# Seven products for two more groups of the first strip, and evictions by a bounded addition and a square

## The chip, the cores and the metric

The kernel runs on one core of a Trainium2 chip. A core has TensorE (matrix products, into the banks of PSUM), VectorE, ScalarE and GpSimd (elementwise work, named DVE, ACT and POOL in the profile), and SyncE (SP), which issues nearly all transfers of this kernel. Each engine has a queue of its own and works through it in order; semaphores tie the queues together. The metric is device time in microseconds, and lower is better. The kernel before took 870.62 us (median of three runs, 869.41 to 871.22).

## The reference

```
kv  = einsum('bhsd,bhse->bhde', k, v)          # batch 8, heads 8, seq 576, head_dim 64
o   = einsum('bhsd,bhde->bhse', q, kv)
rms = sqrt(mean(o * o, axis=-1) + 1e-6)
x   = (o / rms * g_norm) as (4608, 512)        # tokens x (heads * head_dim)
h   = x @ w_in                                 # w_in (512, 2048), given as float64
g   = max(h, 0) ** 2
out = g @ w_out                                # w_out (2048, 512), given as float64
```

All of it is computed in fp32 from k, v, q in fp32. The two products of the feed-forward part are nearly all of the arithmetic.

## The kernel before

**Strips.** The 4608 tokens are worked in 9 strips of 512. For each strip the kernel computes h, squares it and multiplies by w_out ("up" and "down"). Between these products TensorE does the attention of later strips in small slices, in an order that Python code writes out by hand; the compiled order of every engine is the order in which the code emits. TensorE's work is cut down by Strassen's scheme in Winograd's form: a product of 2 x 2 blocks by seven products of sums of blocks instead of eight. Strips 2 to 8 apply it twice, strip 1 once in up and twice in down, strip 0 once in down.

**Strip 0, up.** It uses w_in as it comes, without sums. A group g (of `NG` = 4) holds four tiles, `(fh, i)`; a tile is four matmuls with 512 columns into a bank of its own (`up_first`, tag "f", four banks in rotation), and the group's four quarters of g are the tiles `dest[11]`, `dest[12]`, `dest[21]`, `dest[22]`. ScalarE evicts a tile: relu in place (L916), then a square for each half (L918). Three tiles of group 0 are done in the opening; the other thirteen are the steps i = 3 to 15.

**Weights.** While that goes on the weights arrive as float64 and are converted to fp32 in pairs of pieces. `convert(PACE[i])`, called after each step, says how far. For each pair ScalarE makes two words (L260, L262), GpSimd clamps one (L282), and VectorE puts them together (L284, L288). ScalarE's words of pair n + 1 are emitted with the rest of pair n; a pair's word tile `w_c` has two buffers and its raw tile five. Pairs 2 to 7 are w_in (groups 1 to 3), pairs 8 to 11 quarters of w_out that go into `w_s`, and pairs 12 to 15 the other quarters, of which VectorE also makes sums (`sums_out`, L306), which SP stores to HBM.

**Down of strip 0 and what follows.** At the end of up VectorE makes sums of g (`sum_g1`, L897); `down` then runs the seven products in the order 1, 2, 5, 6, 7, 3, 4. During it ScalarE scales w_in by g_norm and VectorE makes the seven-product sums of w_in for strip 1 (`sums_in`, four operations for a group: a sum and three differences, into `w_s` and over block a21) and the sums of x of strip 1 (`sums_x`, four tiles).

**Seven products (`up`).** For a group the products come in the order 1, 2, 6, 5, 7, 3, 4 (`ORDER`), eight matmul instructions of 256 columns each. They share three banks (`BANK`): A takes 1, 6, 7 and 4, which add up in it, B takes 5 and 3, and C takes 2. `combine` reads a bank between its products: after 1, 6 and 5 ScalarE copies it out (`snap`, L880); after 2, 7 and 3 VectorE adds bank and snapshot into quarters 11, 22 and 12 (L933), and multiplies the result by its positive part (L934); after 4 ScalarE takes bank A by relu and square (L938, L939) into quarter 21. Snapshots lie in the pool "c", six buffers.

```
    ORDER = (1, 2, 6, 5, 7, 3, 4)
    BANK = {1: "A", 6: "A", 7: "A", 4: "A", 5: "B", 3: "B", 2: "C"}
    A_IN = {1: 0, 2: 2, 3: 6, 4: 3, 5: 4, 6: 5, 7: 1}
```

`A_IN` names the block of w_in that a product takes: 0 to 3 are the four blocks themselves, 4 to 6 the sums s1, s2, s4. Attention slices come between: transposes (T), products of keys and values (K), queries (x_ps), norms (root on ScalarE, newton steps and x_n on VectorE) and features.

Of the kernel before, what the change touches and what calls it, by code (L numbers as in the profile page):

```python
# [9 lines left out]

FP32 = mybir.dt.float32
I32 = mybir.dt.int32
# [2 lines left out]
AF = mybir.ActivationFunctionType  # L15
ALU = mybir.AluOpType
# [4 lines left out]
def kernel(  # L21
# [34 lines left out]
    nc = tc.nc  # L56
    P = 128
# [13 lines left out]
    TH = STRIP // 2  # L71
# [4 lines left out]
    SQ = 32  # L76
    Q_ON_PE = 2
    BEHIND = 1.6
    X_ON_PE = 2
    EPS = 1e-6  # L80
    AHEAD = 10
    PACE = (3, 4, 4, 5, 6, 7, 8, 9, 10, 11, 12, 13, 13, 14, 15, 16)
# [9 lines left out]
    c_pool = ctx.enter_context(tc.tile_pool(name="c", bufs=6))  # L92
# [124 lines left out]
    KH, FH, DH = NP // 2, d_ff // 2, d_model // 2  # L217
    FQ = FC // 2
    WN = 512
    NG = FQ // 2  # L220
# [3 lines left out]
    block = lambda b: w_in[:, :, :, b] if b < 4 else w_s[:, :, :, b - 4]  # L224
# [67 lines left out]
    def convert_pair(n, dest):  # L292

        for i in range(acted[0], min(n + 2, len(sources) // 2)):
            convert_pair_on_act(i)
            acted[0] = i + 1
        deque(conversion(pair_words.pop(n), dest, nc.gpsimd), 0)
        load_more(2 * n + 2)
# [6 lines left out]
    def minus(eng, out, a, b):  # L305
        eng.tensor_tensor(out=out, in0=a, in1=b, op=ALU.subtract)  # L306
# [3 lines left out]
    def pieces_in(i):  # L310
        g, k = divmod(i // 2, KH)
        convert_pair(i // 2, w_in[:, k, g].rearrange("p (a b) e -> p a (b e)", a=2))

    def sums_in(g):

        nc.scalar.activation(w_in[:, :, g, 0:4], w_in[:, :, g, 0:4], AF.Copy, scale=g_col)
        a11, a21, a12, a22, s1, s2, s4 = (block(b)[:, :, g] for b in range(7))
        nc.vector.tensor_tensor(out=s1, in0=a21, in1=a22, op=ALU.add)
        minus(nc.vector, s2, s1, a11)
        minus(nc.vector, s4, a12, s2)  # L320
        minus(nc.vector, a21, a11, a21)
# [24 lines left out]
    def convert(n):  # L346
        while converted[0] < min(n, len(conversions)):
            fn, a = conversions[converted[0]]
            fn(a)
            converted[0] += 1  # L350
# [339 lines left out]
    def halves(s, kh, th):  # L690
        return xt[s][:, ts(th, TH // SQ), ts(kh, KH), :]

    def sums_x(s):
        xc[s] = t1, t2, t3, t4 = [
            sum_pool.tile([P, TH // SQ, KH, SQ], FP32, name=f"x_t{i}", tag="sum") for i in range(4)
        ]
        x = lambda kh, th: halves(s, kh, th)
        minus(nc.vector, t1, x(0, 1), x(0, 0))
        minus(nc.vector, t2, x(1, 1), t1)
        minus(nc.vector, t3, x(1, 1), x(0, 1))  # L700
        minus(nc.vector, t4, x(1, 0), t2)
# [99 lines left out]
    def attend_between(slot, begun, goal, late, first, last):  # L801
# [6 lines left out]
        while slice_at[0] < most:  # L808
# [58 lines left out]
    def product(p, i, lhsT, rhs, n):  # L867

        for k in range(n):
            nc.tensor.matmul(  # L870
                bank[BANK[p]][:, i, :], lhsT=lhsT(k), rhs=rhs(k),
                start=p in (1, 5, 2) and i == 0 and k == 0, stop=k == n - 1, skip_group_check=True,
            )
# [46 lines left out]
    def up(s, g, p):  # L920
        open_bank(p)
        rhs = {
            1: halves(s, 0, 0), 2: halves(s, 1, 0), 3: halves(s, 1, 1),
            4: xc[s][3], 5: xc[s][0], 6: xc[s][1], 7: xc[s][2],
        }[p]
        for i in range(2):
            product(p, i, lambda kc: block(A_IN[p])[:, kc, g, ts(i, P)], lambda kc: rhs[:, :, kc, :], KH)
        dest = quarters(s, g)

        def relu_squared(q):  # L930
            def f(b, a):
                o = dest[q]
                nc.vector.tensor_tensor(out=o, in0=b, in1=a, op=ALU.add)  # L933
                nc.vector.scalar_tensor_tensor(out=o, in0=o, scalar=0.0, in1=o, op0=ALU.max, op1=ALU.mult)  # L934
            return f

        def last(b):
            nc.scalar.activation(dest[21], b, AF.Relu)  # L938
            nc.scalar.activation(dest[21], dest[21], AF.Square)  # L939

        combine(p, relu_squared(11), relu_squared(12), last, relu_squared(22))
# [417 lines left out]
    for s in range(N_STRIP):  # L1359
# [7 lines left out]
        if s >= DEEP_UP:  # L1367
            steps = [(0.5, up_slot, (s, slot)) for slot in range(55)]
        elif s == 0:
            steps = [(2, up_first, (g, fh, i)) for g in range(NG) for fh in range(2) for i in range(2)]  # L1370
        else:
            steps = [(1, up, (s, g, p)) for g in range(NG) for p in ORDER]
        n_up = len(steps)
# [6 lines left out]
        if s >= DEEP_UP:  # L1380
            goal = max(goal, min(ready[DEEP_UP] + (len(slices) - ready[DEEP_UP]) * (s - 1) // (N_STRIP - DEEP_UP - 1), len(slices)))
            if s > DEEP_UP:
                goal = min(pair_ends, key=lambda end: abs(end - goal))
        total, done = sum(w for w, _, _ in steps), 0
        for i, (w, fn, a) in enumerate(steps):
            if s == 0 and i < n_up:

                if i == 0:
                    load_next()
                    load_rest(1, nc.sync)  # L1390
                    load_next()
                if i == 1:
                    load_next()
                if i == 2:
                    for b in range(2):
                        load_q_rest(b, nc.sync)
                if i == 14:
                    for b in range(2):
                        store_first(b)
            elif s == 0 and i == n_up:  # L1400
                convert(len(conversions))
                conv.close()

                stream_pool = ctx.enter_context(tc.tile_pool(name="stream", bufs=6, reuse_waits="tile"))
                sum_pool = ctx.enter_context(tc.tile_pool(name="sum", bufs=8, reuse_waits="tile"))
# [6 lines left out]
            fn(*a)  # L1412
            if s == 0 and i < n_up:

                convert(PACE[i])
            done += w
            if s:
                clock[0] += 3.2 if i >= n_up else 2.2 if s == DEEP else 1.2
                soon = tiles_due and tiles_due[0][2][0] // NT == s + 1
                if i == n_up + 10:  # L1420
                    while tiles_due and tiles_due[0][2][0] // NT == s + 1:
                        _, f, a = tiles_due.popleft()
# [35 lines left out]
                sums_in((7, 8, 9, 12).index(i - n_up))  # L1458
            if i == n_up + 11:
                sums_x(1)  # L1460
            n = i + 1 - (n_up - 6)
            pairs, m = divmod(max(n - 2 * NP, 0), 3)
            attend(min(ready[0] + min(max(n, 0), 2 * NP) + (n >= 2 * NP) + 4 * pairs + (0, 2, 2)[m], goal))
            while deep_due and i not in (n_up + 1, n_up + 4, n_up + 12, n_up + 13):
# [38 lines left out]
```

## Time and profile before

| | |
|---|---|
| median of three runs | 870.62 us |
| the profiled execution | 868.8 us, span 867.0 us |
| TensorE busy | 857.8 us (99%) |
| VectorE, ScalarE, GpSimd busy | 702.0, 348.9, 328.1 us |
| granted TensorE clock | 1.000 |
| a plain tile of strip 0, start to start | 3.43 us (8 instructions) |
| a product of 256 columns in up, start to start | 1.73 us (8 instructions) |
| up of strip 0 after the opening | 33.6 to 82.4 us |
| down of strip 0 | 83.1 to 138.2 us |
| up of strip 1 | 138.25 to 195.1 us |

In the timelines a line gives start, duration, engine, line of the kernel, operation, and what is written from what; a bracket at the end gives how long the engine was idle before and what ended that. A matmul in fp32 is two instructions, and consecutive ones overlap, so the distance from start to start is the price and not the duration. ScalarE is busy for 12.9, 12.4 and 14.8 of 15 us in the stretches 30 to 45, 45 to 60 and 60 to 75 us, VectorE for 8.8, 8.6 and 12.0 there and for 14.8 and 14.6 in the next two.

### The profile page before, as it was taken

The page shows a single profiled execution, that of the slowest core. Times are in us where ns is not written, and L with a number is a line of the kernel's source. Part 1 is how long each engine was busy: PE and PEld are TensorE (multiplying, and loading weights), DVE is VectorE, ACT ScalarE, POOL GpSimd, SP SyncE. Part 2 cuts the span into 40 slices and gives each one's busy share as a digit, 9 for nine tenths or more (in the row PEclk, how much of TensorE's full clock was granted, in tenths as well). Part 3 has the DMA queues.
Part 4 walks back from the last instruction along what each step waited for, and adds up shares of the span by engine and source line. Part 5 has one row for each costly group of instructions (what it writes and reads, how often), then busy time and mean ns, then how long its engine had stood idle before and what let it go on. Part 6 is the DMA issues. An engine that isn't in the chain of part 4 may idle for free.

```text
span 867.0 us, 32426 instructions
## 1 busy us (share of the span) xinstructions
PE 857.8 (99%) x14176; PEld 804.2 (93%) x14176; DVE 702.0 (81%) x1132; ACT 348.9 (40%) x777; POOL 328.1 (38%) x335
## 2 busy tenths in 40 slices
PE   7999999999999999999999999999999999999998
PEld 6445888889999999999999999999999999999998
DVE  3768988879877996789688967897889777975887
ACT  4888241320048303750356034901491148102810
POOL 1223004630458223730574045704470447145700
PEclk9999999999999999999999999999999999999999
DMA  9898998999999997989698979987678856885583
GB/s 307 277 362 269 274 377 239 295 332 353 280 264 259 342 325 233 228 307 344 209 244 273 341 239 281 283 297 270 198 236 302 301 165 221 293 282 196 175 315 121
DMA packets 169469, 236.46 MB, mean 273 GB/s; under 512 B 78704, under 2 KB 133744, under 8 KB 161008
## 3 DMA queue, kind: packets, MB, share of 16 engines
q1 hardware_dynamic: 169024, 234.33, 83.5%
q8 instruction: 111, 1.82, 0.9%
q14 instruction: 30, 0.25, 0.1%
q10 hardware_dynamic: 304, 0.07, 0.0%
HBM read 197.66 MB, written 36.70 MB: 270 GB/s over the span
## 4 chain that ended last, share of the span: by engine, by line
PE 83%; DMA 7%; DVE 5%; ACT 3%; SPq 1%; issue 1%; DVEq 0%; ACTq 0%
PE ps_A L865 36%; PE ps_B L865 31%; PE ps_C L865 5%; PE ps_A L870 4%; DMA raw<-in_moe_w_in_dram 2%; PE kv_ps L448 2%; PE x_ps L484 2%; PE ps_B L870 2%; DVE w_t L306 1%; DMA w_deep<-w_t 1%; DMA raw<-in_moe_w_out_dram 1%; DMA w_blk<-w_deep 1%; PE ps_C L870 1%; DMA first_qkv<-in_v_dram 1%; ACT w_c L260 1%
## 5 line engine op out<-in xcount | busy, mean ns | idle before, releaser
L865 PE MATMUL ps_B<-w_blk,g_s 128*64 128x128 f32 x2016 | 122.0, 273 | 0.0
L865 PEld LDWEIGHTS ps_B<-w_blk,g_s 128*64 128x64 f32 x2016 | 112.6, 137 | 0.1
L306 POOL TENSOR_TENSOR x_l<-xT 128x256 f32<-128x256 f32 x21 | 16.2, 773 | 230.2 <-PE ps_A L865 230.2
L865 PE MATMUL ps_B<-w_blk,gt 128*64 128x128 f32 x1504 | 94.1, 273 | 0.3 <-DMA w_blk<-w_deep 0.3
L865 PE MATMUL ps_A<-w_blk,g_s 128*64 128x128 f32 x1536 | 92.2, 273 | 0.0
L1323 POOL TENSOR_TENSOR snap<-snap,gt 128x512 f32<-128x512 f32 x35 | 46.2, 1320 | 112.5 <-ACT snap L1328 93.6
L865 PEld LDWEIGHTS ps_A<-w_blk,g_s 128*64 128x64 f32 x1536 | 85.7, 137 | 0.0
L865 PEld LDWEIGHTS ps_B<-w_blk,gt 128*64 128x64 f32 x1504 | 84.6, 137 | 0.8 <-PE ps_B L865 0.5
L1328 ACT COPY snap<-ps_A 128x512 f32<-128x512 f32 x63 | 36.8, 585 | 103.6 <-PE ps_A L865 96.2
L1263 ACT ACTIVATE gt<-gt 128x512 f32<-128x512 f32 x112 | 70.2, 627 | 9.9 <-DVE gt L1323 9.9
L1264 ACT ACTIVATE gt<-gt 128x512 f32<-128x512 f32 x112 | 70.7, 631 | 3.5
L865 PE MATMUL ps_A<-w_blk,gt 128*64 128x128 f32 x1152 | 71.2, 273 | 0.0
L865 PEld LDWEIGHTS ps_A<-w_blk,gt 128*64 128x64 f32 x1152 | 64.7, 137 | 0.0
L1112 ACT COPY o_sb<-ps_A 128x128 f32<-128x128 f32 x24 | 6.4, 265 | 144.7 <-PE ps_A L865 109.4
L306 DVE TENSOR_TENSOR gt<-gt 128x2048 f32<-128x2048 f32 (+1 forms) x29 | 59.7, 2063 | 0.0
L1111 DVE TENSOR_TENSOR o_sb<-o_sb,ps_B 128x256 f32<-128x256 f32 (+1 forms) x123 | 47.4, 386 | 14.3 <-ACT o_sb L1112 9.5
L865 PE MATMUL ps_A<-x_l,w_in 128*64 128x128 f32 x896 | 58.6, 273 | 0.2 <-DVE gt L1323 0.2
L1323 POOL TENSOR_TENSOR gt<-gt,snap 128x512 f32<-128x512 f32 x42 | 52.5, 1279 | 15.1 <-DVE snap L1323 15.1
L865 PEld LDWEIGHTS ps_A<-x_l,w_in 128*64 128x64 f32 x896 | 50.8, 137 | 0.5 <-DVE gt L1323 0.5
L865 PE MATMUL ps_B<-x_l,w_blk 128*64 128x128 f32 x784 | 51.2, 273 | 0.0
L865 PE MATMUL ps_A<-x_l,w_blk 128*64 128x128 f32 x784 | 51.2, 273 | 0.0
L1112 ACT COPY o_sb<-ps_B 128x128 f32<-128x128 f32 x31 | 8.2, 265 | 96.3 <-PE ps_B L865 96.3
(214 smaller groups left out, 1900.2 us busy)
## 6 DMA issues: line engine op xcount, KB each, us to landing
w_blk<-w_deep SPq DMA_DIRECT2D x56, 1024.0 KB, 7.3
w_blk<-w_out SPq DMA_DIRECT2D x56, 768.0 KB, 6.2
w_blk<-w_in_deep SPq DMA_DIRECT2D x49, 768.0 KB, 5.8
raw<-in_moe_w_in_dram SPq DMA_DIRECT2D x16, 512.0 KB, 9.2
raw<-in_moe_w_out_dram SPq DMA_DIRECT2D x16, 512.0 KB, 8.0
k<-in_k_dram SPq DMA_DIRECT2D x29, 256.0 KB, 4.9
v<-in_v_dram SPq DMA_DIRECT2D x29, 256.0 KB, 5.2
x_d<-x_q SPq DMA_DIRECT2D x27, 256.0 KB, 4.8
```

Of the source, the lines that this page charges most:

```text
L260: nc.scalar.activation(c, high_f, AF.Copy, scale=EXPONENT)
L306: eng.tensor_tensor(out=out, in0=a, in1=b, op=ALU.subtract)
L448: nc.tensor.matmul(ps[ts(h, D), i], lhsT=a, rhs=w, start=i == 0 and c == 0, stop=c == C, skip_group_check=True)
L484: nc.tensor.matmul(ps[half, r, i, ts(p, D)], lhsT=q[row, half], rhs=kvd[b, p][row, row], start=True, stop=True)
L865: nc.tensor.matmul(ps[half], lhsT=lhsT[:, half], rhs=rhs, start=start, stop=stop, skip_group_check=True)
L870: nc.tensor.matmul(bank[BANK[p]][:, i, :], lhsT=lhsT(k), rhs=rhs(k), start=p in (1, 5, 2) and i == 0 and k == 0, stop=k == n - 1, skip_gro ...
L1111: add = lambda out, a, b: nc.vector.tensor_tensor(out=out, in0=a, in1=b, op=ALU.add)
L1112: yield nc.scalar.copy(q[:, 3:4], small(1))
L1263: nc.scalar.activation(o, o, AF.Relu)
L1264: nc.scalar.activation(o, o, AF.Square)
L1323: add = lambda eng, out, a, b: eng.tensor_tensor(out=out, in0=a, in1=b, op=ALU.add)
L1328: nc.scalar.copy(t, ps)
```

## The change

Groups 2 and 3 of strip 0 (`PLAIN` = 2) are computed by the seven products of `up`. The sums of x that it needs are made by `sums_x(0)` in four buffers of the pool "c", ahead of step 5's conversion; the sums of w_in, unscaled since strip 0's x carries g_norm, by `first_sums_in`, for group 2 ahead of step 6's conversion and for group 3 after the fourth product of group 2 (product 5) and the conversion behind it. Because `w_s` is filled with w_out at that time, s1, s2 and s4 are put into the group's own quarters 22, 12 and 21, which the products' evictions overwrite later; a11 - a21 goes over a21. `sums_in` then has three operations for groups 2 and 3, starting from that difference. The steps of strip 0's up are 8 tiles and 14 products; the variable `at` maps a product's step to one of the sixteen turns, so that loads, conversions and attention slices keep to the turns.

The evictions change in strip 1 (quarters 11, 22 and 12) and in strip 0 for quarter 12: one operation of VectorE adds bank and snapshot and bounds the sum from below by zero (`TENSOR_ADD_SAT`), and ScalarE squares it in place. In strip 0 quarters 11 and 22 keep the two operations of VectorE.

```diff
+    first_w = {}
+    def first_sums_in(g):
+        a11, a21, a12, a22 = (block(b)[:, :, g] for b in range(4))
+        dest = quarters(0, g)
+        s1, s2, s4 = first_w[g] = [dest[q] for q in (22, 12, 21)]
+        nc.vector.tensor_tensor(out=s1, in0=a21, in1=a22, op=ALU.add)
+        minus(nc.vector, s2, s1, a11)
+        minus(nc.vector, s4, a12, s2)
+        minus(nc.vector, a21, a11, a21)
...
     def sums_in(g):
...
+        if g >= PLAIN:
+            minus(nc.vector, s2, a22, a21)
+            nc.vector.tensor_tensor(out=s1, in0=s2, in1=a11, op=ALU.add)
+            minus(nc.vector, s4, a12, s2)
+            return
...
     def sums_x(s):
+        pool, tag = (sum_pool, "sum") if s else (c_pool, "c")
         xc[s] = t1, t2, t3, t4 = [
-            sum_pool.tile([P, TH // SQ, KH, SQ], FP32, name=f"x_t{i}", tag="sum") for i in range(4)
+            pool.tile([P, TH // SQ, KH, SQ], FP32, name=f"x_t{i}", tag=tag) for i in range(4)
         ]
...
         for i in range(2):
-            product(p, i, lambda kc: block(A_IN[p])[:, kc, g, ts(i, P)], lambda kc: rhs[:, :, kc, :], KH)
+            b = A_IN[p]
+            w = first_w[g][b - 4] if s == 0 and b > 3 else block(b)[:, :, g]
+            product(p, i, lambda kc: w[:, kc, ts(i, P)], lambda kc: rhs[:, :, kc, :], KH)
...
                 o = dest[q]
+                if s or q == 12:
+                    nc.vector._custom_dve(TENSOR_ADD_SAT, out=o, in0=b, in1=a, s0=float("inf"), s1=0.0)
+                    nc.scalar.activation(o, o, AF.Square)
+                    return
                 nc.vector.tensor_tensor(out=o, in0=b, in1=a, op=ALU.add)
                 nc.vector.scalar_tensor_tensor(out=o, in0=o, scalar=0.0, in1=o, op0=ALU.max, op1=ALU.mult)
...
-            steps = [(2, up_first, (g, fh, i)) for g in range(NG) for fh in range(2) for i in range(2)]
+            steps = [(2, up_first, (g, fh, i)) for g in range(PLAIN) for fh in range(2) for i in range(2)]
+            steps += [(1, up, (s, g, p)) for g in range(PLAIN, NG) for p in ORDER]
...
+        plain, turns = 4 * PLAIN, 4 * NG
         for i, (w, fn, a) in enumerate(steps):
-            if s == 0 and i < n_up:
+            if s == 0:
+                before, at = at, i if i < plain else plain + (i - plain) * (turns - plain) // (n_up - plain)
+                if i >= n_up:
+                    at = turns + i - n_up
+            if s == 0 and at < turns and at > before:
...
             fn(*a)
             if s == 0 and i < n_up:
-                convert(PACE[i])
+                if i == plain - 3:
+                    sums_x(0)
+                if i == plain - 2:
+                    first_sums_in(PLAIN)
+                if at > before:
+                    convert(PACE[at])
+                if i == plain + 3:
+                    first_sums_in(PLAIN + 1)
```

More of the change, by code (lines that the diff above doesn't have):

```diff
@@ L9 @@
 from concourse._compat import with_exitstack
+from concourse.dve_ops import TENSOR_ADD_SAT
 FP32 = mybir.dt.float32
@@ L78 @@
     BEHIND = 1.6
+    PLAIN = 2
     X_ON_PE = 2
@@ L1383 @@
                 goal = min(pair_ends, key=lambda end: abs(end - goal))
-        total, done = sum(w for w, _, _ in steps), 0
+        total, done, at = sum(w for w, _, _ in steps), 0, -1
+        plain, turns = 4 * PLAIN, 4 * NG
         for i, (w, fn, a) in enumerate(steps):
-            if s == 0 and i < n_up:
+            if s == 0:
[3 more added lines that the diff above has]
+            if s == 0 and at < turns and at > before:
                 if i == 0:
@@ L1396 @@
                         load_q_rest(b, nc.sync)
-                if i == 14:
+                if at == 14:
                     for b in range(2):
@@ L1460 @@
                 sums_x(1)
-            n = i + 1 - (n_up - 6)
+            n = at + 1 - (turns - 6)
             pairs, m = divmod(max(n - 2 * NP, 0), 3)
```

## The prediction

> **What bounds the kernel now.** I read the page's totals first, then TensorE's timeline over 20 to 200 us, then the list of waits of TensorE, then the timelines of ScalarE and VectorE over the same stretch. The totals say that the product engine is the bound:
>
> ```profile
> span 867.0 us, 32426 instructions
> ...
> PE 857.8 (99%) x14176; PEld 804.2 (93%) x14176; DVE 702.0 (81%) x1132; ACT 348.9 (40%) x777; POOL 328.1 (38%) x335
> ```
>
> TensorE's timeline gives the price of both ways to compute a group, and the one wait that this stretch has:
>
> ```profile
> 51.08 3.60 PE L911 MATMUL ps_A<-xT,w_in 128*128 128x512 f32 x8
> 54.51 3.60 PE L911 MATMUL ps_B<-xT,w_in 128*128 128x512 f32 x8
> ...
> 83.06 3.72 PE L870 MATMUL ps_A<-w_s,gt 128*128 128x256 f32 x16
> ...
> 131.24 7.17 PE L870 MATMUL ps_A<-w_blk,gt 128*128 128x256 f32 x32 [0.46 <-DVE o_sb L1042]
> ...
> 149.22 1.89 PE L870 MATMUL ps_B<-xT,w_s 128*128 128x256 f32 x8
> 150.95 1.89 PE L870 MATMUL ps_A<-x_t,w_in 128*128 128x256 f32 x8
> ```
>
> A plain tile follows the last after 3.43 us (four to a group), a product after 1.73 us (seven to a group). ScalarE in the same stretch runs about five microseconds behind TensorE:
>
> ```profile
> 55.47 0.59 ACT L916 ACTIVATE ps_C<-ps_C 128x512 f32<-128x512 f32 x1
> 56.09 0.66 ACT L918 ACTIVATE gt<-ps_C 128x256 f32<-128x256 f32 x2
> 57.53 1.16 ACT L260 ACTIVATE w_c<-raw 128x1024 f32<-128x1024 f32 x1 [0.78 <-DMA raw<-in_moe_w_out_dram]
> 58.58 1.15 ACT L262 ACTIVATE raw<-raw 128x1024 int32<-128x1024 uint32 x1
> 59.61 0.60 ACT L916 ACTIVATE ps_A<-ps_A 128x512 f32<-128x512 f32 x1
> ```
>
> The tile that TensorE began at 51.08 and left at 54.68 is evicted at 59.61, behind the words of a weight pair whose transfer lands at 57.4. Plain tiles bear this: each has a bank to itself, and four banks go round. VectorE:
>
> ```profile
> 55.68 1.23 DVE L284 SCALAR_TENSOR_TENSOR w_c<-w_c,raw 128x1024 int32<-128x1024 int32 x1 [2.31 <-POOL w_c L282]
> ...
> 72.61 1.41 DVE L306 TENSOR_TENSOR w_s<-wt,w_s 128x512 f32<-128x512 f32 x1
> 74.06 0.69 DVE L306 TENSOR_TENSOR wt<-wt,w_s 128x512 f32<-128x512 f32 x1
> ...
> 149.49 0.69 DVE L933 TENSOR_TENSOR gt<-ps_A,snap 128x512 f32<-128x512 f32 x1 [2.26 <-PE ps_A L870]
> 150.22 1.39 DVE L934 SCALAR_TENSOR_TENSOR gt<-gt 128x512 f32<-128x512 f32 x1
> ...
> 152.99 1.13 DVE L516 SCALAR_TENSOR_TENSOR newton<-newton,rms 128x8 f32<-128x8 f32 x1
> ...
> 155.94 0.68 DVE L933 TENSOR_TENSOR gt<-ps_B,snap 128x512 f32<-128x512 f32 x1
> ```
>
> It has gaps until 70 us (after 46: 1.41, 0.93, 2.31, 1.68, 0.93, 0.93, 0.93, together 9.1) and none from 70.1 to 109.7.
>
> **Strip 0, TensorE's own work.** Two groups of 4 x 3.43 = 13.7 become 7 x 1.73 = 12.1: 3.3 us saved. From the start of group 2 (51.08) to the first product of the down projection (83.06) TensorE now takes 32.0 us. Afterwards its work there is 14 x 1.725 = 24.2, plus batch 1's transposes and key products between, 3.6 by their spacings, plus 0.2: 28.0 if nothing waits.
>
> **Strip 0, the new waits.** Products 1, 6, 7, 4 add into one bank, and between them the bank is read: ScalarE's snapshot of product 1 must end before product 6 starts, that of 6 before 7, VectorE's eviction of quarter 22 before 4. I laid the queues out in the changed kernel's compiled order at the durations of the rows.
> - Snapshot 1 of group 2 stands in ScalarE's queue where the eviction at 59.61 stood: behind the words of pair 9. Ready 59.6, done 60.2 (a copy is 0.59). Product 6 could start at 54.5: TensorE waits 5.7. The sums that it also needs are ready: x sums at 46.1 to 48.7, weight sums at 51.2 to 53.9, in VectorE's gaps.
> - VectorE then has pair 9 (59.84 to 62.4), quarter 11 (two operations, 1.33), pair 10 (2.5), group 3's four weight sums (2.65), and only then quarter 22, done 70.2. Product 4 could start at 67.6: 2.65.
> - The square of quarter 12 is on ScalarE and waits for VectorE's new addition, which stands behind pair 11 (70.2 to 72.7) and ends at 73.4. Queued behind that square: relu and square of quarter 21 (1.2), pair 13's words (2.1), a kv copy, snapshot 1 of group 3, done 78.4. Product 6 of group 3 could start at 76.75: 1.7. Its product 4 waits 0.4 for quarter 22.
>
> Together 10.4; 28.0 + 10.4 = 38.4 against 32.0: TensorE reaches the down projection 6.4 us late. At 131.24 it waited 0.46 for VectorE; that goes: **+6.0**.
>
> Does VectorE bind as well? Added: 4 sums of x, 8 of weights (0.60 to 0.72 each), 4 evictions of two operations (1.33), 2 of one (0.69): 14.5 us. The gaps take 8.2 of the 9.1, so from 75 to 109 it runs 5 to 7 us late, about like TensorE: the first sum of g, ready at 93.2 for a product at 99.88, is ready at 98.4 to 100 for one at 106.3; the addition that gated 131.24 is 5.2 to 5.6 late. So a shorter wait on ScalarE would not win it back: with pair 9 landed three microseconds earlier the same layout still gives +5.6. Stores of w_out, pieces and their loads, and the deep sums keep SP's order and move with VectorE, less than TensorE does. POOL's clamps follow ScalarE's words; nothing else waits for POOL before 142.
>
> ScalarE loses 8 tiles' evictions (1.17 by spacing, 9.4 us) and gains 6 snapshots and 6 relus and squares (7.1): its total falls, its place in the chain does not.
>
> **Strip 1.** The scaled sums of groups 2 and 3 take three operations for four (1.2 us of VectorE), the twelve L934 go (0.69 to 1.72 each) and twelve squares (0.6) come to ScalarE. TensorE has no wait on VectorE between 138 and 195, so what VectorE saves is worth nothing there; what counts is the new order. Times of before: quarter 22's addition at 149.49 now ends at 150.2; its square and then the root (L507), behind it on ScalarE, end at 151.1, and the newton steps, x_n and a weight sum, 4.4 us from 151.53 to 155.94, start then. Quarter 12's addition: 155.5 to 156.2. ScalarE holds, behind its square (0.6), relu and square of 21 (1.2) and snapshot 1 of the next group (0.6): 158.6, for a product 6 due at 156.56. **+2.0**. Without POOL beside them the newton rows at 1.01 and 1.13 are 0.17, which makes it 0.3; if the new additions take as long as L934 beside POOL (1.4), 3.5. The later groups have VectorE on time and cost under 0.3.
>
> **Prices that no row shows.** The new operation (addition with bounds, one input in PSUM): L933 has the same operands and is 0.65 to 0.69 in all twelve; L934 reaches 1.72. I take 0.69, the nearer. Sums of two SBUF inputs: 0.69, but 1.41 where a clamp of POOL runs (72.3 to 73.5); twelve new ones, and clamps run in 12 of the 42 us from 46 to 88: 0 to 12 x 0.72 x 0.29 = 2.5 us. I take 0, since the timeline shows most such sums at 0.69. The squares and snapshots have rows.
>
> [...] The granted clock is full in all 40 slices, and TensorE's longest wait in this trace is 1.4 us, so no row shows what 5.7 us do. [...]
>
> **Sum.** The profiled execution took 868.8 for its span of 867.0. 868.8 + 6.0 + 2.0 = 876.8. It lies 1.8 below the median of the runs shown (870.62), so the forecast for a median is 878.6.
>
> **Rivals.**
> - *Strip 1 is free* (newton steps short, as their other rows are): 876.6. For it: at 170 us the same steps take 0.17 each. Against: POOL works from 142 to 160 as before.
> [...]
> - *Faster*: the words of pairs 8 to 10 are no longer held by evictions, run ahead, and snapshots come on time, so VectorE's additions fill gaps and the 3.3 us stay: 867.3. It decides at 55.1 us: pair 9's piece would have to land by then (54.5 + 3.3 less words 2.1 and copy 0.6) instead of 57.4, and VectorE's 14.5 us would have to fit the gaps. Against: ScalarE already stood idle for that transfer, whose issue is unmoved; VectorE alone gives +5.6.
> - *No change*: waits and savings cancel near 3.3: 870.6.
>
> **Chances.** Forecast 0.50, strip 1 free 0.25, dearer 0.13, faster 0.08, no change 0.04. A median of this kernel moves by some 0.2% (1.7 us) by itself. So slower by more 0.88, within 0.04, faster 0.08. The range leaves out faster, no change and the far end of dearer: 874.0 to 883.0, with strip 0 at +3.4 and strip 1 free at the low end and strip 0 at +8 with strip 1 at +4.4 at the high.
>
> **What would show it.** In TensorE's waits: ps_A on ScalarE's snapshot about 5.7 near 54.5 and 1.7 near 77, ps_A on VectorE's gt about 2.7 near 68; the first w_s product near 89.5 instead of 83.06; the first product of strip 1 near 144.2; a wait of about 2 us for a snapshot near 162. The new operation at 0.69. I am wrong if snapshot 1 of group 2 starts before 57, if VectorE still has gaps at 75 us, or if TensorE takes back time after 145.

## The result, and the profile after

The changed kernel took 890.48 us (median of four runs, 889.98 to 891.52), the kernel before 870.85 us beside it (869.41 to 871.22). The ratio is 1.023, with a 95% interval of 1.0212 to 1.0248. The change costs 2.3%, about 20 us; the forecast was slower by 8.

In the traces the span went from 867.0 to 888.3 us. Where the 21.3 us arise can be read off at four places of TensorE's order that both kernels pass: the first product of the down projection of strip 0, the first and the second block of queries in strip 1 (x_ps), and the end.

| | before | changed | later by |
|---|---|---|---|
| down projection of strip 0 begins | 83.06 | 93.71 | 10.7 |
| first query block of strip 1 | 141.8 | 152.1 | 10.3 |
| second query block of strip 1 | 161.6 | 180.4 | 18.8 |
| span | 867.0 | 888.3 | 21.3 |

So 10.3 us come from strip 0 and 8.5 from one short stretch of strip 1 (28.3 us between the two blocks instead of 19.8). The opening, which the change does not touch, differs from execution to execution: the first tile behind it starts at 33.6 us in the trace of before, at 32.1 in this one, and between 31.5 and 34.8 in all traces of this case. The totals of the page:

```profile
span 888.3 us, 32533 instructions
PE 861.4 (97%) x14224; PEld 817.2 (92%) x14224; DVE 706.9 (80%) x1140; ACT 353.2 (40%) x777; POOL 328.2 (37%) x335
```

TensorE's busy time rose by only 3.6 us, and its share fell from 99 to 97%: most of the loss is waiting. TensorE's timeline of strip 0, groups 2 and 3:

```profile
49.59 1.89 PE L890 MATMUL ps_A<-xT,w_in 128*128 128x256 f32 x8
...
60.78 3.78 PE L890 MATMUL ps_A<-x_t,gt 128*128 128x256 f32 x8 [7.58 <-ACT snap L900]
64.36 1.98 PE L890 MATMUL ps_B<-x_t,gt 128*128 128x256 f32 x8
...
73.04 1.99 PE L890 MATMUL ps_A<-x_t,w_in 128*128 128x256 f32 x8 [2.81 <-DVE gt L959]
...
81.58 1.99 PE L890 MATMUL ps_A<-x_t,gt 128*128 128x256 f32 x8 [1.73 <-ACT snap L900]
...
91.06 1.99 PE L890 MATMUL ps_A<-x_t,w_in 128*128 128x256 f32 x8 [0.94 <-DVE gt L959]
...
93.71 3.72 PE L890 MATMUL ps_A<-w_s,gt 128*128 128x256 f32 x16
```

The four waits that the prediction listed are all there, in the places that it gave: 7.58, 2.81, 1.73 and 0.94 us. The first product after the longest of them takes twice its time (3.58 us to the next start instead of 1.73): the granted clock is 0.50 from 60.8 to 64.3. VectorE's timeline of the same stretch:

```profile
66.98 1.94 DVE L290 SCALAR_TENSOR_TENSOR w_s<-raw,w_c 128x1024 int32<-128x1024 int32 x1
...
70.28 1.50 DVE L308 TENSOR_TENSOR gt<-w_in,gt 128x512 f32<-128x512 f32 x1
...
72.31 0.68 DVE L959 TENSOR_TENSOR gt<-ps_A,snap 128x512 f32<-128x512 f32 x1
...
102.37 2.49 DVE L917 TENSOR_TENSOR g_s<-gt 128x512 f32<-128x512 f32 x4
```

Product 4 at 73.04 waits for the addition of quarter 22 at 72.31, and that stands behind the weight sums of group 3. Between 46 and 102 us VectorE has a single gap (0.9 us, where the kernel before has 9.1). Two of the operations shown, at 66.98 and 70.28, take 0.7 to 0.8 us longer than their like, and a clamp of GpSimd runs beside each:

```profile
66.33 1.51 POOL L284 TENSOR_SCALAR w_c<-w_c 128x1024 f32<-128x1024 f32 x1 [2.92 <-ACT w_c L262]
70.20 1.04 POOL L284 TENSOR_SCALAR w_c<-w_c 128x1024 f32<-128x1024 f32 x1 [2.35 <-ACT w_c L262]
```

The kernel before has three such long operations in this stretch, 2.3 us above their like in all; here it is nine, 6.8 us in all. The first sum of g starts at 102.37 instead of 92.58. In strip 1, TensorE, VectorE and ScalarE:

```profile
174.35 1.98 PE L467 MATMUL kv_ps<-v,k 128*64 128x64 f32 x32 [5.60 <-ACT xT L674]
...
176.68 3.78 PE L890 MATMUL ps_B<-x_t,w_s 128*128 128x256 f32 x8
```

```profile
171.27 0.71 DVE L419 STREAM_TRANSPOSE qT<-q 128x512 f32<-128x512 f32 x1 [6.03 <-DMA q<-in_q_dram]
...
172.48 0.68 DVE L956 CUSTOM_DVE_ANT_0 gt<-ps_C,snap 128x512 f32<-128x512 f32 x1
```

```profile
173.19 0.63 ACT L957 ACTIVATE gt<-gt 128x512 f32<-128x512 f32 x1 [6.87 <-DVE gt L956]
173.73 0.57 ACT L674 COPY xT<-xt_ps 128x512 f32<-128x512 f32 x1
```

Back along the chain: ScalarE's square of quarter 11 of group 1 (L957) waits 6.87 us for VectorE's addition (L956); that stands behind a query transpose (L419) that waits 6.03 us for its transfer; behind the square stands ScalarE's copy of features (L674), for which TensorE's products of keys and values wait 5.60 us. These products and product 5 then run on a granted clock of 0.50: 174.35 to 176.68 takes 2.33 us and product 5 3.71 (1.31 and 1.93 at 158.39 and 159.70 in the kernel before). Wait and clock together are 5.6 + 2.8 = 8.4 of the 8.5 us. In the kernel before, VectorE waits for the same transfer, for 2.91 us, and TensorE waits for nothing there:

```profile
161.82 0.71 DVE L400 STREAM_TRANSPOSE qT<-q 128x512 f32<-128x512 f32 x1 [2.91 <-DMA q<-in_q_dram]
```

### The profile page after: what moved, and what is told of

Read it like the earlier page. It is cut to its first block, busy times and chain, and to the rows that moved or that the text cites. A ratio compares the mean times of both kernels' runs of the same rounds, so it can differ in the third digit from the quotient of the medians.

```text
span 888.3 us, 32533 instructions
## 1 busy us (share of the span) xinstructions
PE 861.4 (97%) x14224; PEld 817.2 (92%) x14224; DVE 706.9 (80%) x1140; ACT 353.2 (40%) x777; POOL 328.2 (37%) x335
## 3 DMA queue, kind: packets, MB, share of 16 engines
q8 instruction: 112, 1.84, 0.9%
## 4 chain that ended last, share of the span: by engine, by line
PE 85%; DMA 4%; DVE 3%; SPq 3%; ACT 2%; issue 1%; DVEq 0%; ACTq 0%
PE ps_A L885 35%; PE ps_B L885 30%; PE ps_A L890 6%; PE ps_C L885 5%; PE ps_B L890 3%; PE kv_ps L467 2%; PE x_ps L503 2%; DMA raw<-in_moe_w_in_dram 2%; PE ps_C L890 1%; DVE w_c L286 1%; DMA q_rest<-in_q_dram 1%; DMA w_blk<-w_deep 1%; SPq L128 1%; SPq L250 1%; DMA v<-in_v_dram 1%
## 5 line engine op out<-in xcount | busy, mean ns | idle before, releaser
L885 PE MATMUL ps_B<-w_blk,gt 128*64 128x128 f32 x1504 | 96.0, 273 | 2.1 <-DMA w_blk<-w_deep 1.6
L1095 DVE TENSOR_TENSOR g_s<-gt 128x512 f32<-128x512 f32 x56 | 46.1, 823 | 0.7 <-ACT gt L957 0.7
```

What stands on the lines that cost most here:

```text
L885: nc.tensor.matmul(ps[half], lhsT=lhsT[:, half], rhs=rhs, start=start, stop=stop, skip_group_check=True)
L1095: nc.vector.tensor_tensor(out=t, in0=a21, in1=a22, op=ALU.add)
```

## The experiments

Two theories were put to the test. S: strip 1 loses its time because ScalarE's square of quarter 11 stands ahead of the copy of features and waits, through VectorE, for a query transfer. V: strip 0 loses its time because VectorE has too much to do; its rival W puts the same loss on ScalarE's queue, as the prediction had. A second pair, B and P, is on whether less work on TensorE is worth anything in strip 0. The ratios are to runs of the kernel before on the same chip; its medians there were 869.92, 868.38 and 869.51 us in the three sets. "Above before" is the ratio times these. The expectations count from 870 to 871 us for the kernel before, so it is the amounts above before that can be compared with them. "Come back" is measured from the changed kernel at 1.023; such a difference is known to about 3 us.

### Strip 1: its evictions, alone, undone, and put later

Strip 1's evictions as before, strip 0 as changed:

```diff
-                if s or q == 12:
+                if not s and q == 12:
```

> Strip 0 as in the changed kernel, strip 1's evictions as before (two operations of VectorE, none of ScalarE). In the changed kernel's trace strip 0 starts its down projection 10.3 us late and strip 1 loses 8.5 more between its first and its second block of queries (152.1 to 180.4 us), where TensorE waits 5.6 us for ScalarE's copy of features. Theory S: that wait comes from strip 1's own evictions (ScalarE's square of quarter 11 stands ahead of the copy and waits for VectorE, which waits 6.0 us for a query transfer). Then all of the 8.5 goes: the wait for the copy is gone and the time is 880 to 882.5. Rival R: strip 1 suffers because strip 0 came late and transfers bunched, whatever the evictions: 888 to 891.

Measured: 882.3 us (879.6 to 883.8), ratio 1.0123 (1.0086 to 1.0161), 10.7 us above before. From the first to the second query block it is 19.8 us again, and no wait for the copy is left. Without the evictions of strip 1 nothing of that loss is left; strip 0's lateness alone does not cause it.

The same evictions in the kernel before, where strip 0 is on time:

```diff
-                nc.vector.tensor_tensor(out=o, in0=b, in1=a, op=ALU.add)
-                nc.vector.scalar_tensor_tensor(out=o, in0=o, scalar=0.0, in1=o, op0=ALU.max, op1=ALU.mult)
+                nc.vector._custom_dve(TENSOR_ADD_SAT, out=o, in0=b, in1=a, s0=float("inf"), s1=0.0)
+                nc.scalar.activation(o, o, AF.Square)
```

> The kernel before with strip 1's evictions alone changed to one addition with a lower bound and ScalarE's square; strip 0 as before. Theory S: the query transfer lands at the same time, near 161.5, VectorE waits for it 5 to 6 us instead of 2.9, ScalarE's copy of features is 5 to 7 us late and TensorE waits about 5 us there: 877.5 to 880.5 (7 to 9.5 above before). Rival R: without strip 0's delay there is no bunching: within 1.5 us of before, 869.5 to 872.5.

Measured: 875.19 us (870.9 to 878.5), ratio 1.0058 (1.0036 to 1.0079): 5.0 us above before (3.1 to 6.9), less than the 7 to 9.5 that theory S gave and more than the rival's 1.5. The trace of one execution (875.3 us) has the same chain, with 26.8 us between the blocks: 7.0 more than before, where the changed kernel has 8.5. TensorE:

```profile
157.62 1.99 PE L871 MATMUL ps_A<-x_t,w_s 128*128 128x256 f32 x8 [1.45 <-ACT snap L881]
163.18 1.15 PE L449 MATMUL kv_ps<-v,k 128*64 128x64 f32 x32 [3.57 <-ACT xT L656]
...
164.54 3.58 PE L871 MATMUL ps_B<-x_t,w_s 128*128 128x256 f32 x8
```

The wait at 163.18 is the one seen above, 3.6 us instead of 5.6: here VectorE waits 3.6 us for the query transfer and not 6.0. The first line is the wait for a snapshot behind a square that the prediction had put at 2.0 us; it is 1.45 here, and in the changed kernel it is not there: the newton steps ahead of it took 0.17 us each, here two of the three take 0.75 and 1.12.

The changed kernel with ScalarE's squares of strip 1 two products later in its queue:

```diff
-                    nc.scalar.activation(o, o, AF.Square)
+                    unsquared.append([2 if s and g < NG - 1 else 0, o])
...
+        while unsquared and unsquared[0][0] <= 0:
+            o = unsquared.pop(0)[1]
+            nc.scalar.activation(o, o, AF.Square)
+        for u in unsquared:
+            u[0] -= 1
```

> The changed kernel with strip 1's squares (groups 0 to 2) put two products later in ScalarE's queue, behind the copy of features and the copies of keys and values; VectorE's work stays as in the changed kernel. Theory S says that only the place in the queue matters: 880 to 882.5, as with the old evictions, and no wait for the copy of features. Rival R, and a rival that the new operation itself is what costs: 888 to 891.

Measured: 883.57 us (880.2 to 885.9), ratio 1.0138 (1.0102 to 1.0174), 12.0 us above before, and 19.8 us between the blocks. The median lies above the range given; the mechanism is as theory S has it. VectorE still waits for the query transfer, longer than ever, and ScalarE no longer with it:

```profile
170.35 0.71 DVE L419 STREAM_TRANSPOSE qT<-q 128x512 f32<-128x512 f32 x1 [6.62 <-DMA q<-in_q_dram]
```

```profile
166.06 0.59 ACT L674 COPY xT<-xt_ps 128x512 f32<-128x512 f32 x1 [1.05 <-PE xt_ps L673]
```

The same in the kernel before, to see what the evictions are worth when they stand in nobody's way:

```diff
-                nc.scalar.activation(o, o, AF.Square)
+                unsquared.append([2 if g < NG - 1 else 0, o])
```

> The kernel before with strip 1's new evictions alone, ScalarE's squares two products later in its queue (groups 0 to 2). Theory S: without the square ahead of the copy of features nothing is lost, and as TensorE waits for VectorE nowhere in strip 1 nothing is won: within 1 us of before. Rival (the new operation or ScalarE's additional work costs by itself): 4 to 6 us above before, as with the squares in place.

Measured: 868.45 us (867.2 to 874.0), ratio 0.9986 (0.9962 to 1.0010). Neither a loss nor a gain that can be told from none, as expected: no cost of the operation itself or of the twelve squares shows (the interval ends at 0.9 us), and what cost 5.0 us was the place in ScalarE's queue. No gain from what it saves VectorE shows either, in a strip where TensorE does not wait for VectorE.

### Strip 0: VectorE's queue or ScalarE's

The changed kernel without the twelve sums of x and w_in in strip 0:

```diff
-        s1, s2, s4 = first_w[g] = [dest[q] for q in (22, 12, 21)]
-        nc.vector.tensor_tensor(out=s1, in0=a21, in1=a22, op=ALU.add)
-        minus(nc.vector, s2, s1, a11)
-        minus(nc.vector, s4, a12, s2)
-        minus(nc.vector, a21, a11, a21)
+        first_w[g] = a11, a12, a22
...
-                    sums_x(0)
+                    xc[0] = [halves(0, kh, th) for kh in range(2) for th in range(2)]
```

> The changed kernel without VectorE's twelve sums of x and of w_in in strip 0 (the products take the blocks themselves in place of the sums, so strip 0's output is another): some 10 us of VectorE's work go, nothing else moves. Theory V: VectorE's queue sets strip 0's pace (it has no gap over 1 us from 48 to 102 us in the changed kernel): the wait for quarter 22 of group 2 (2.8 us) goes, and what is left is the wait for the first snapshot, so the down projection starts near 88 instead of 93.7 and the time is 884 to 886. Rival W: ScalarE's queue sets it (the first snapshot behind the words of pair 9, and squares): the down projection starts at 92 or later and the time is 888.5 to 890.5.

Measured: 885.18 us (883.7 to 886.1), ratio 1.0158 (1.013 to 1.0186), 13.7 above before: 6.3 us come back, for sums of 9 to 10 us. In TensorE's timeline the wait ahead of product 4 of group 2 is gone and the down projection begins at 88.78, as theory V gave.

```profile
59.05 3.78 PE L886 MATMUL ps_A<-xT,w_in 128*128 128x256 f32 x8 [5.59 <-ACT snap L896]
...
68.56 1.89 PE L886 MATMUL ps_A<-xT,w_in 128*128 128x256 f32 x8
...
88.78 3.72 PE L886 MATMUL ps_A<-w_s,gt 128*128 128x256 f32 x16
```

Some 5.7 us of strip 0 stay even so, with a wait of 5.59 us for snapshot 1: with VectorE relieved, ScalarE's queue is the next to bind. Whether VectorE's other operations beside the clamps are shorter here, too, is not shown, so the 6.3 us may hold more than the sums themselves.

The first snapshot ahead of the words of pair 9:

```diff
-                if at > before:
+                if at > before and i != plain - 1:
                     convert(PACE[at])
```

> The changed kernel with the first snapshot of group 2 ahead of the words of pair 9 in ScalarE's queue (the conversion of pair 8, which emits those words, is written behind product 1). VectorE's work is the same. The wait of 7.6 us ahead of product 6 goes. Theory V (VectorE's queue sets strip 0's pace): quarter 22 of group 2 is ready no earlier, TensorE waits that much longer for it, product 4 still starts at 72.5 to 73.5, the down projection at 93 to 94.5, and the time is 889 to 891. Theory W (ScalarE's queue sets it): product 7 starts at about 63.5 instead of 66.2, the down projection at 91 or earlier, and the time is 886 to 888.

Measured: 889.22 us (885.7 to 893.0), ratio 1.0234 (1.0202 to 1.0266): no change against 1.023.

```profile
55.11 1.99 PE L890 MATMUL ps_A<-x_t,gt 128*128 128x256 f32 x8 [1.97 <-ACT snap L900]
...
61.82 3.64 PE L890 MATMUL ps_A<-x_t,w_in 128*128 128x256 f32 x8 [2.99 <-ACT snap L900]
...
71.75 3.56 PE L890 MATMUL ps_A<-x_t,w_in 128*128 128x256 f32 x8 [3.80 <-DVE gt L959]
...
92.43 3.72 PE L890 MATMUL ps_A<-w_s,gt 128*128 128x256 f32 x16
```

The wait of 7.58 us became 1.97, and products 6 and 5 start 5.7 and 7.4 us earlier; then TensorE waits 2.99 for snapshot 6 and 3.80 for quarter 22 and begins the down projection 1.3 us earlier (theory V had given at most 0.7, theory W 2.7 or more). Of the largest wait of the prediction at most 1.3 us were on the path in this trace, and none shows in the time.

TensorE kept busy instead of waiting:

```diff
+            if s == 0 and i == plain + 2:
+                ps = apsum.tile([P, C, P], FP32, name="t_ps", tag="at")
+                keep_busy(ps[:, 0], 56)
             fn(*a)
```

> The changed kernel with 56 small matmuls of the identity ahead of product 6 of group 2, into a bank that nobody reads, so that TensorE is busy in the 7.6 us in which it waits for the snapshot. The half clock behind that wait should go: product 6 follows its own spacing of 1.73 us instead of 3.58. Theory V: these 1.85 us are hidden by the wait for quarter 22 (2.8 us becomes 4.7), product 4 starts at 73 as before, and the time is unchanged, 889 to 891. Rival, that the half clock is on the path: the down projection comes 1.9 us earlier, 887.5 to 888.7.

Measured: 888.89 us (two runs, 887.6 and 890.2), ratio 1.0229 (1.0194 to 1.0264). Two runs cannot tell no change from the rival's 2 us, but the trace can.

```profile
52.43 12.67 PE L411 MATMUL t_ps<-ident 128*128 128x128 f32 x112
64.93 1.89 PE L890 MATMUL ps_A<-x_t,gt 128*128 128x256 f32 x8
66.66 1.89 PE L890 MATMUL ps_B<-x_t,gt 128*128 128x256 f32 x8
...
72.28 1.89 PE L890 MATMUL ps_A<-x_t,w_in 128*128 128x256 f32 x8
...
92.75 3.72 PE L890 MATMUL ps_A<-w_s,gt 128*128 128x256 f32 x16
```

The 56 matmuls took 12.5 us, more than the wait that they were to fill, so product 6 started 4.2 us later than in the changed kernel, now at the full clock (1.73 us to the next). Product 4 nevertheless starts at 72.28, and the down projection at 92.75, 0.8 and 1.0 us earlier than in the changed kernel, where group 2 also began 0.6 us later. Four microseconds of delay on TensorE cost nothing there, and the half clock behind the long wait (1.85 us) cost at most a few tenths.

GpSimd's clamp of the weight words left out after the opening:

```diff
-        yield eng.tensor_scalar(out=c, in0=c, scalar1=MOST, scalar2=-MOST, op0=ALU.min, op1=ALU.max)
+        if eng is not None:
+            yield eng.tensor_scalar(out=c, in0=c, scalar1=MOST, scalar2=-MOST, op0=ALU.min, op1=ALU.max)
...
-        deque(conversion(pair_words.pop(n), dest, nc.gpsimd), 0)
+        deque(conversion(pair_words.pop(n), dest, None), 0)
```

> The changed kernel without GpSimd's clamp of each weight pair after the opening (the step that bounds the exponent of the float64 words; ScalarE's words go to VectorE as they are). In the changed kernel nine of VectorE's operations between 46 and 90 us take 0.7 to 0.8 us longer than their like, 6.8 us in all, each beside such a clamp. If the clamp causes that (one of two engines waiting for the other's access) and theory V holds, all of these operations fall to their shorter time, the first sum of g starts near 95.5 instead of 102.4, the down projection near 88, and the time is 883.5 to 886.5. If the clamps are not the cause, those operations stay long and the time stays within 1 us of 890.

Measured: 884.3 us (883.2 to 885.3), ratio 1.0172 (1.0145 to 1.0199), 14.9 above before: 5.0 us come back. Not one of the nine long operations is long, the first sum of g starts at 96.00, and the down projection at 88.41. The second step of the conversion of pair 10, which is 1.94 us long at 66.98 in the changed kernel (L290, here L291), and the first sum of g:

```profile
64.42 1.22 DVE L291 SCALAR_TENSOR_TENSOR w_s<-raw,w_c 128x1024 int32<-128x1024 int32 x1
...
96.00 2.49 DVE L918 TENSOR_TENSOR g_s<-gt 128x512 f32<-128x512 f32 x4
```

So the long operations beside GpSimd's clamps, priced at nothing in the forecast, are worth about as much as strip 0 cost above it. Leaving out the clamp also shortens the way from ScalarE's words to VectorE, so that a part of the 5.0 us may be that. The 5.0 and the 6.3 us above need not add up: without the clamps the sums are short as well (0.69 us each; in the changed kernel two of the twelve take 1.41 and 1.50).

### What the saving in strip 0 is worth, and one group alone

The kernel before with four matmuls of 512 columns left out, 3.43 us of TensorE's work and nothing else:

```diff
-            for kc in range(NP):
+            n = NP - 1 if g >= 2 and i else NP
+            for kc in range(n):
```

> The kernel before, with one of the four 512-column matmuls left out in half of the tiles of groups 2 and 3 of strip 0 (four in all, 3.43 us of TensorE's time; strip 0's output is another). It takes away what the seven products would take away, and adds nothing to any engine. Theory B (the saving is worth its size): 866.5 to 868 if before is at 870. Theory P (TensorE is not what paces strip 0's end: at 131.24 it waits 0.46 us for VectorE's additions, which do not come earlier): the wait at the end of the down projection grows from 0.5 to about 3.9 us, and the time stays within 1 us of before.

Measured: 868.88 us (867.0 to 875.2), ratio 1.0003 (0.9975 to 1.003). No gain shows, where theory B had given 2 to 3.4 us; the interval still admits 2.2. The profiled execution happens to be the slowest of the twelve (875.2), with its losses after 240 us; strip 0 in it:

```profile
49.86 3.60 PE L912 MATMUL ps_A<-xT,w_in 128*128 128x512 f32 x8
...
68.88 0.66 PE L417 MATMUL t_ps<-ident,q 128*128 128x128 f32 x4 [2.03 <-ACT qT L422]
...
80.56 3.72 PE L870 MATMUL ps_A<-w_s,gt 128*128 128x256 f32 x16
...
129.80 7.17 PE L870 MATMUL ps_A<-w_blk,gt 128*128 128x256 f32 x32 [1.27 <-DVE o_sb L1043]
```

Group 2 starts 1.2 us earlier than in the kernel before (49.86, 51.08), which is the opening's doing, and the last product of the down projection 1.4 us earlier (129.80, 131.24). So of the 3.43 us only 0.2 are left there. The trace shows where most of the rest went. TensorE waits 2.03 us for ScalarE's copy of a query block, where the kernel before waits 0.29:

```profile
70.07 0.66 PE L417 MATMUL t_ps<-ident,q 128*128 128x128 f32 x4 [0.29 <-ACT qT L422]
```

It also waits 0.34 us for a copy of keys and values, and 1.27 for VectorE where it was 0.46: together 2.9 us more than before. Theory P named the last of these waits alone; the larger part is ScalarE's queue, where the copy stands right behind the words of a weight pair. The kernel with strip 1's evictions alone, whose strip 0 is that of before, agrees: its group 2 began 1.2 us earlier than in the kernel before (49.91), TensorE waited 1.62 us for the same copy, and the down projection began at 83.23.

Group 2 alone by seven products, the first snapshot ahead of the words of pair 9, all evictions with VectorE's two operations (the edit's main lines):

```diff
+            steps += [(1, up, (s, PLAIN, p)) for p in ORDER]
+            steps += [(2, up_first, (PLAIN + 1, fh, i)) for fh in range(2) for i in range(2)]
```

> Group 2 of strip 0 alone by seven products, group 3 plain, every eviction with VectorE's two operations as before, and the first snapshot ahead of the words of pair 9. TensorE's own work falls by 1.65 us; VectorE gains four sums of x, four of w_in and three evictions, 5.5 + 4.1 us by their rows, nearly all before 72 us, where the kernel before has 9.1 us of gaps. Theory V: what counts is whether this fits in the gaps: if it does, 868.0 to 870.0; with sums stretched beside GpSimd's clamps some 2 us stay, 870 to 873. Theory W: snapshot 6 behind the words of pairs 9 and 10 still holds product 7 for 6 us: 873 to 876.

Measured: 874.25 us (873.4 to 875.9), ratio 1.0062 (1.0042 to 1.0081), 5.4 us above before.

```profile
56.55 3.50 PE L890 MATMUL ps_A<-x_t,gt 128*128 128x256 f32 x8 [2.59 <-ACT snap L900]
...
62.82 1.99 PE L890 MATMUL ps_A<-x_t,w_in 128*128 128x256 f32 x8 [0.86 <-ACT snap L900]
...
66.94 1.99 PE L890 MATMUL ps_B<-xT,gt 128*128 128x256 f32 x8 [1.68 <-ACT snap L900]
...
69.28 1.99 PE L890 MATMUL ps_A<-x_t,w_in 128*128 128x256 f32 x8 [0.35 <-DVE gt L959]
```

The time is the one that theory W gave, but not by the wait that it named: product 7 waits 0.86 us for snapshot 6 and not 6. Waits of 2.59, 0.86, 1.68 and 0.35 us, 1.57 for the clock after the first (3.30 to the next start), less the 1.65 saved, make 5.4; 5.1 of the waits are for snapshots. VectorE's first sum of g is 4.1 us late (96.66). Whether the words on ScalarE set the time is what the next kernel asks.

The same group with conversions and words behind its snapshots and evictions (the edit's main lines, against the changed kernel):

```diff
-                if at > before and i != plain - 1:
+                if i < plain - 1:
                     convert(PACE[at])
+                elif i != plain + 4 and i >= plain + 3:
+                    convert((9, 0, 10, 11, 12, 13, 14, 15)[i - plain - 3])
```

> Group 2 alone by seven products, with the conversion of pair 8 and the words of pair 9 behind the third snapshot, and the later conversions behind VectorE's evictions of the group, so that no eviction waits for a transfer. The waits for snapshots (2.6, 0.9 and 1.7 us in the other order) go. Theory B: what is left is TensorE's 1.65 us, 867.5 to 869.5 if before is at 870. Theory P: VectorE has 9.6 us more to do ahead of its additions for the down projection and 9.1 us of gaps, so that the wait at the end of the down projection takes the saving back: 869.5 to 873.

Measured: 875.04 us (871.1 to 878.4), ratio 1.0054 (1.0031 to 1.0077), 4.7 us above before and 2 us above theory P's range. In the trace, of an execution of 871.6 us (2.8 above that of before), one wait for a snapshot is left, and after the start of the down projection, at 81.89, TensorE waits for VectorE:

```profile
55.41 1.99 PE L890 MATMUL ps_A<-x_t,gt 128*128 128x256 f32 x8 [2.32 <-ACT snap L900]
...
103.39 1.31 PE L673 MATMUL xt_ps<-ident,x_n 128*128 128x128 f32 x8 [1.07 <-DVE x_n L598]
...
110.85 7.17 PE L890 MATMUL ps_A<-w_blk,gt 128*128 128x256 f32 x32 [1.60 <-DVE gt L308]
```

A feature tile waits 1.07 us for VectorE's x_n and a product 1.60 for a difference of quarters of g. The down projection begins 1.2 us earlier than in the kernel before, but group 2 began 1.6 us earlier (49.48): the stretch between takes 32.4 us, 32.0 in the kernel before, so the 1.65 us saved are lost to the first wait already. 2.32 + 1.07 + 1.60 - 1.65 is 3.3 us, which accounts for the profiled execution; what the others of these runs lose beyond it is open. With most of the snapshot waits gone the time is nearly the same (4.7 us against 5.4, the intervals overlap), and VectorE's first sum of g starts at 96.66 as in the kernel ahead. So with one group neither queue alone sets the time: where ScalarE's words are moved, VectorE's lateness is the next to show.

## Why the prediction was right and wrong

- **Direction and places: right.** Slower was given 0.88. The four waits of strip 0 came where the prediction put them: 5.7, 2.65, 1.7 and 0.4 us were forecast, 7.58, 2.81, 1.73 and 0.94 measured. The first is longer mostly because group 2 began 1.5 us earlier in this execution (49.59); it ends at 60.7, forecast 60.2. That it ends there is partly luck: the forecast has pair 9's words wait for their transfer, and in the trace they wait for VectorE (1.45 us, until 57.96). Without the clamps it is VectorE that waits for those words (1.32 us, until 59.44). The new operation was taken at 0.69 and measures 0.68 (172.48).
- **Strip 0 as a sum: wrong, +6.0 forecast, about +10.7 measured (strip 0 alone, by ratio; 7.5 to 14.0).** The term mis-sized is "I take 0" for VectorE's operations stretched beside GpSimd's clamps. With an upper bound of 2.5 us it was set at nothing because most such sums in the trace of before are short. It was 4.5 us more than before (6.8 against 2.3): the bound counted the twelve new sums alone, and of the nine long operations only two are such sums; four are the conversions L286 and L290, which VectorE's filled gaps brought beside the clamps. VectorE's addition of quarter 22 of group 2 ended at 73.0 us, where the forecast had the quarter done at 70.2. Without the clamps 5.0 us come back.
- **Which queue sets strip 0: named second, should have been first.** The prediction built the sum on ScalarE's late snapshot, and had "VectorE alone gives +5.6" as a check. VectorE's lateness is the cause: 9.8 us at the first sum of g, against 5 to 7 forecast. Taking the first snapshot's wait away, or making TensorE 4 us later, changed nothing that shows in the time; relieving VectorE gave 5.0 and 6.3 us. What is left then, 4.4 to 5.7 us, is about what the forecast's sum had for ScalarE's waits; the step that failed is that VectorE's lateness would not add to them.
- **The saving of 3.3 us: not a gain to begin with.** The sum counted TensorE's own work at 28.0 us instead of 32.0. Four matmuls less, with nothing added, are worth 0.3 us the wrong way (2.2 gained to 2.6 lost). One row that spoke for it stood in the prediction, TensorE's wait for VectorE at 131.24. Another was overlooked: the prediction calls that the one wait of the stretch, but at 70.07 TensorE waits 0.29 us for ScalarE's copy, and this is the wait that takes half of the saving (1.74 of 3.43 us).
- **Strip 1: wrong, +2.0 forecast, 8.5 measured.** The step that failed is "The later groups have VectorE on time and cost under 0.3". The prediction followed ScalarE's new wait for VectorE through group 0 alone. In the kernel before, VectorE waits 2.91 us for the query transfer of the transpose at 161.82, ahead of the eviction of quarter 11 of group 1, harmless as ScalarE did not wait for that eviction. The predicted wait of 2.0 did not occur in the changed kernel, and came out as 1.45 in the one with strip 0 on time and long newton steps.
- **"What VectorE saves is worth nothing there": right**, as far as the evictions with late squares show (0.9986, 0.9962 to 1.0010). VectorE came earlier to the same transfer and only waited longer for it, 4.37 us there.
- **The clock after the long wait: not in the sum.** As the prediction says, no row of before shows what 5.7 us do, and its 878.6 holds nothing for it. After the wait of 7.58 us product 6 took 3.58 us instead of 1.73 (granted clock 0.50 from 60.8 to 64.3); product 5 ran at full speed again (1.81). In strip 0 next to nothing of it shows in the time (the kernel kept busy is as slow); in strip 1, where the prediction had no wait for the copy of features, the half clock cost 2.8.
- **Rivals.** "Faster" needed pair 9's piece by 55.1 and VectorE's work to fit its gaps; the words began at 57.99, waiting for VectorE, and one gap of 0.9 us was left, so its second condition failed. "Strip 1 is free" had its own condition met (newton steps of 0.17) and failed on the chain that was not listed. "Dearer" (0.13) came nearest: VectorE's operations beside GpSimd's clamps did grow dearer, by 4.5 us, while the new operation stayed at 0.68. No row gives the +8 of strip 0 at the high end of the range; about +10.7 was measured. Of the three signs of being wrong none appeared: they watched strip 0's first snapshot, VectorE at 75 us and a gain after 145, and the loss came elsewhere.
- **Open.** The remaining 2 to 3 us of the span, after 180 us, lie mainly in two waits for weight blocks (1.62 us at 307.7 and 0.41 at 302.4); the other kernels' profiled executions lose between 0.3 and 8.1 us behind the third query block of strip 1, in different places, and none of these runs isolates it.

## What to carry to other kernels

Before an operation is moved to another engine's queue, follow every instruction that will stand behind it there, in all repetitions, back to the transfers that its producer waits for: here a wait that was harmless on VectorE became TensorE's once ScalarE stood in line behind it, and with the square two products further back it cost nothing that shows. Before TensorE's work in a stretch is cut, leave some of it out and measure: where the order is tied to another engine's queue, less work there may buy nothing, while the sums that pay for it are on the path. When VectorE's gaps were filled up it also met GpSimd's clamps more often, so that its older operations grew dearer as well as the new ones (nine long ones instead of three, 6.8 us above their like instead of 2.3): price the old ones again too.

## What was not expected of the hardware

- **Half clock after short waits.** After waits of 2.59, 2.99, 3.80, 5.59 and 7.58 us a product of TensorE took 3.3 to 3.6 us to the next start instead of 1.73; after 2.81, 2.32, 1.97 and 1.73 us it took 1.92, 1.84, 1.83 and 1.92. In the changed kernel the granted clock is 0.50 behind the 7.58 us (60.8 to 64.3) and 1.00 behind the 2.81 us (73.04 to 74.9). So the length of the wait alone does not decide: after 2.59 us a product took 3.30, after 2.81 us 1.92. What decides besides is not shown. After 3.57 us in the kernel with the evictions alone, the key products still ran at 1.15 us and product 5, 1.4 us later, took 3.51 us to the next start (1.93 in the kernel before).
- **VectorE beside GpSimd.** A step of a conversion (SCALAR_TENSOR_TENSOR on 128x1024) takes 1.23 us alone and 1.94 to 2.06 in the four cases where it is long beside a clamp, a sum of 128x512 0.69 and 1.41 to 1.52. A clamp takes 1.04 us while VectorE is idle (54.60 in the kernel before) and up to 2.02 beside a step: that one (59.23 in the changed kernel) left the step beside it at 1.22. Without clamps none of VectorE's nine operations is long. Their long and short times differ by 0.7 to 0.8 us; how the two engines hold each other up is not shown.
